# Six chunk lengths between 500 and 512 in place of five of 512 and one of 480, in a column attention followed by a two-layer block on one TensorE-bound core

## The chip, the cores and the metric

The kernel runs on one core of one Trainium2 chip. The metric is the device time of one execution in microseconds (us), from the start to the end of the program on that core; the time before is the median of three runs. A profiled execution gives, beside that, the time of each instruction on each engine: TensorE (PE, whose weight loads are listed apart as PEld), VectorE (DVE), ScalarE (ACT), GpSimd (POOL) and SyncE (SP), which issues the DMAs.

## The reference

```python
def _attn_ref(q, k, v, tau):                      # each (4, 6080, 256)
    qn = q / (np.linalg.norm(q, axis=1, keepdims=True) + 1e-06)
    kn = k / (np.linalg.norm(k, axis=1, keepdims=True) + 1e-06)
    s = kn.transpose(0, 2, 1) @ qn / tau          # (4, 256, 256)
    s = s - s.max(-1, keepdims=True)
    a = np.exp(s)
    a /= a.sum(-1, keepdims=True) + 1e-09
    return (v @ a).astype(np.float32)             # (4, 6080, 256)

def _moe_ref(x, w_in, w_out):                     # (24320, 256), (256, 2048), (2048, 256)
    h = x @ w_in
    g = h - np.tanh(h)
    return (g @ w_out).astype(np.float32)
```

The attention's result, reshaped to 24,320 tokens, is the second function's input. There are four batches of 6,080 tokens.

## The kernel before

**The algebra.** For each batch the 256 by 256 scores are made first. The softmax matrix is then multiplied into `w_in` (`fold`, tile `ps_w`), eight pieces of 256 hidden columns, so that `v` times the folded weight gives the hidden layer at once. That product is done by a seven-product scheme for two by two blocks (Winograd's form of Strassen's): the two columns of blocks on the moving side are two *chunks* of tokens, x and y, and the two rows are the two halves of the 256 channels. A *pair* of chunks of equal length `n` is therefore the unit of the work on tokens. All operands of these products are split into a high and a low part of a four-byte format with reduced precision, and each product takes three matmuls (high by low, high by high, low by high).

**Loops.** A batch is `NP = 6` pairs (list `pairs`, of start and length `n`), and a pair goes through `NS2 = 8` *slots*, one for each piece of the hidden layer. `gs` numbers the slots through all batches (192 in all). In a slot class `Quad` issues the seven products of the first layer (`products`, L288, tiles `x`, `y`, `z`; 21 matmuls of `n` columns), ACT and DVE add them up and apply h - tanh(h) (L805 to L845, tiles `u`, `p`, `c`, `t`, `gh`, `gl`), and `second` (L905, tiles `ps_o`) issues 24 matmuls of `n` columns into four accumulators that live through the eight slots. So a slot has 45 matmuls of `n` columns each, whatever `n` is. At the end of a pair the four accumulators are copied (L929) and written to `outT` (L940).

**Beside the slots.** Class `Moving` loads a pair's four blocks of `v` (`vraw`, L674), makes the sums (`vt`, L681 and L684) and splits all seven moving operands (L693 on ACT, L696 on DVE) some five slots before the pair begins. The next batch's scores (L288, tile `ps_s`, matmuls of 256 columns) and folds (`ps_w`, 256 columns) are strewn between the slots.

**Buffers.** Tiles for chunks are allocated for `NMAX = 512` columns whatever `n` is, and a shorter chunk uses the first `n` columns of each; a PSUM bank holds 512 columns of four bytes.

**What sets the order.** Class `Plan` records every operation with an estimated cost (`pe_cost`, `act_cost`, `dve_cost`, `pool_cost`, all linear in the number of columns), simulates the engines greedily with these costs, and issues the operations in the order of their simulated starts. The PE's own operations stay in the order in which they were recorded, but for the fills (parts of batch 1's scores), which may move among them. On the host, `kernel` lays out `v` so that a pair's four blocks lie side by side in a row of `v4`.

```python
s0 = 0
while s0 < N:
    n = min(NMAX, (N - s0) // 2)
    pairs.append((s0, n))
    s0 += 2 * n
```

With N = 6,080 this gives five pairs of 512 and one of 480.

Of the kernel before, what the change touches and what calls it, by code (L numbers as in the profile page):

```python
# [18 lines left out]
P = 128  # L19
GJ = 2  # L20
NMAX = 512
NSQ = 760
F64_LEAST = float(np.int32(0x38100000).view(np.float32))

# [204 lines left out]
def attn_moe(ctx: ExitStack, tc: tile.TileContext, qk, v4, qkT, tau, w_in, w_out, outT):  # L229
# [7 lines left out]
    B, N, _, C = qk.shape  # L237
# [3 lines left out]
    FB = 2 * P  # L241
    NJ = N // P
    TAIL = N - NJ * P
    pairs = []
    s0 = 0
    while s0 < N:
        n = min(NMAX, (N - s0) // 2)
        pairs.append((s0, n))
        s0 += 2 * n
    NP = len(pairs)  # L250
    SLOTS = NP * NS2
    TOTAL = B * SLOTS
# [17 lines left out]
    def sb(pool, tag, shape, dtype, name):  # L270
        return pool.tile(list(shape), dtype, tag=tag, name=name, bufs=ring[tag].bufs)

    def bank(i, name, shape=(P, 512)):

        return ps_p.tile(list(shape), F32, tag=f"bank{i}", name=name)
# [38 lines left out]
    class Convert:  # L314
# [10 lines left out]
        def magnitude(self):  # L325
            words = self.raw.rearrange("p a (n w) -> p (a n) w", w=2)
            self.low, self.high = words[:, :, 0], words[:, :, 1]
            self.a = sb(nt_p, "nt", [P, NSQ], I32, f"a_{self.name}")[:, 0:WN]
            self.af = self.a.bitcast(F32)
# [60 lines left out]
    while j < NJ:  # L390
        n = min(GJ, NJ - j) if j else NJ % GJ or GJ
# [7 lines left out]
    class Attn:  # L399
# [25 lines left out]
        def square_plain(self, g):  # L425
            j0, n, rows = groups[g]
            raw = self.parts[g]
            if g == 0:

                self.acc = [bank(i, f"acc{i}_{self.b}", (P, 2, C)) for i in (4, 3)]  # L430
                self.acc.append(sb(g_p, "t", [P, NMAX], F32, "acc").rearrange("p (x c) -> p x c", x=2))
                for a in self.acc[n:]:
# [14 lines left out]
        def take_squares(self, j):  # L447
            sq = sb(g_p, "u", [P, NMAX], F32, f"sq{j}").rearrange("p (x c) -> p x c", x=2)
            nc.scalar.copy(sq, self.acc[j])
            self.acc[j] = sq  # L450
# [25 lines left out]
        def split_hi(self, g):  # L476
            j0, n, rows = groups[g]
            raw = self.parts[g][0]
            hi = sb(qk_p, "qh", [P, GJ, 2, C], F32R, f"qh_{self.b}_{g}")
            nc.scalar.copy(hi[:rows, 0:n], raw[:rows, 0:n])  # L480
            self.parts[g] = [hi, raw]
# [26 lines left out]
        def load_channels(self, i):  # L508

            row, part = divmod(i, N // NSQ)  # L510
            self.channels[i] = sb(nt_p, "nt", [P, NSQ], F32, f"nt_{self.b}_{i}")
            nc.sync.dma_start(
                self.channels[i],
                qkT[row // KC, self.b, row % KC * P:(row % KC + 1) * P, part * NSQ:(part + 1) * NSQ],
            )

        def square(self, i):
            if i == 0:
                self.squares = sm_p.tile([P, 2 * KC, N // NSQ], F32, name="squares")
            x = self.channels.pop(i)  # L520
            row, part = divmod(i, N // NSQ)
            nc.scalar.activation(x, x, AF.Square, accum_out=self.squares[:, row, part:part + 1])
# [138 lines left out]
    class Moving:  # L661
# [9 lines left out]
        def load(self):  # L671
            n, s0 = self.n, self.s0
            self.raw = sb(v_p, "vraw", [P, 4, NMAX], F32, f"vraw_{self.b}_{self.p}")
            nc.sync.dma_start(self.raw[:, :, 0:n], v4[self.b, :, 2 * s0:2 * s0 + 4 * n].rearrange("p (a n) -> p a n", a=4))  # L674

        def sums(self, i):
            n = self.n
            r = self.raw[:, :, 0:n]
            if i == 0:
                self.t = sb(v_p, "vt", [P, 4, NMAX], F32, f"vt_{self.b}_{self.p}")  # L680
                nc.vector.tensor_sub(self.t[:, 0:2, 0:n], r[:, 1:3, :], r[:, 0:2, :])  # L681
# [8 lines left out]
        def split_hi(self, i):  # L690
            x = sb(v_p, "vhl", [P, 2, NMAX], F32R, f"v{i}_{self.b}_{self.p}")
            self.hi[i], self.lo[i] = (x[:, j, 0:self.n] for j in range(2))
# [466 lines left out]
    for gs in range(TOTAL):  # L1159
# [3 lines left out]
        for name, then in ORDER:  # L1163
# [6 lines left out]
            for x in then:  # L1170
                if isinstance(x, int):
                    lag, x = max(0, lag - x), max(0, x - lag)
# [48 lines left out]
```

## Time and profile before

| what | value |
|---|---|
| median of three runs | 2171.79 us (2171.21 to 2172.72) |
| profiled execution, first to last instruction | 2170.3 us |
| around that span (median less span) | 1.5 us |
| PE busy | 2160.4 us, 10,042 matmul records |
| DVE busy | 1750.3 us |
| ACT busy | 1529.9 us |
| mean granted TensorE clock | 0.998 |

The page gives no whole time of the profiled execution apart from its span, so sums made on the trace are set against 2170.3 us, and the difference is carried over to the median. Matmuls overlap, and the duration listed for one is longer than its share of the engine: what a matmul costs in a stream is read from the distance between starts in the timeline, and is called its *pitch* here.

### The profile page before, as it was taken

How to read it: one execution, taken by the hardware profiler on the slowest of the kernel's cores; microseconds unless marked ns; L12 is line 12 of the kernel's file. 1: busy time of each engine (PE TensorE's matmuls, PEld its weight loads, DVE VectorE, ACT ScalarE, POOL GpSimd, SP SyncE). 2: the span in 40 equal slices, each digit the busy share in tenths (PEclk: the TensorE clock that was granted, in tenths of full speed). 3: DMA queues.
4: the chain of work that ended last, by engine and by line, in shares of the span. 5: the costliest groups of instructions: out<-in, count | busy, mean ns of one | idle time of the engine just before them, and what ended most of it. 6: DMA issues, size and time to landing. Idle time of an engine off the chain costs nothing.

```text
span 2170.3 us, 28452 instructions
## 1 busy us (share of the span) xinstructions
PE 2160.4 (100%) x10042; PEld 1818.0 (84%) x10042; DVE 1750.3 (81%) x2844; ACT 1529.9 (70%) x2755; POOL 33.0 (2%) x31
## 2 busy tenths in 40 slices
PE   8999999999999999999999999999999999999999
PEld 7888888888888888888888888888888888888887
DVE  8888877888888777778788877877878878778776
ACT  6566778776777777776677767777667766666665
POOL 5100000000000000000000000000000000000000
PEclk9999999999999999999999999999999999999999
DMA  9844444443454444543345445454333342332331
GB/s 389 330 166 154 164 168 148 162 154 105 151 209 151 172 164 168 182 160 140 126 145 187 170 162 189 143 189 167 128 134 128 122 148 88 129 129 93 125 120 53
DMA packets 82783, 342.23 MB, mean 158 GB/s; under 512 B 9042, under 2 KB 13138, under 8 KB 80082
## 3 DMA queue, kind: packets, MB, share of 16 engines
q1 hardware_dynamic: 82642, 340.43, 43.3%
q8 instruction: 79, 1.29, 0.2%
q14 instruction: 62, 0.51, 0.1%
HBM read 281.94 MB, written 58.46 MB: 157 GB/s over the span
## 4 chain that ended last, share of the span: by engine, by line
PE 98%; DMA 1%; DVE 0%; SPq 0%; issue 0%; ACT 0%
PE ps_o L905 48%; PE x L288 24%; PE y L288 12%; PE ps_s L288 6%; PE z L288 6%; PE ps_w L288 2%; DMA qh<-qk_dram 0%; DMA vhl<-qk_dram 0%; PE ps_n L457 0%; DVE m_wi L346 0%; PE ps_b L564 0%; PE ps_t L599 0%; DVE acc L445 0%; DVE a_wi L339 0%; SPq L323 0%
## 5 line engine op out<-in xcount | busy, mean ns | idle before, releaser
L288 PE MATMUL x<-v,f 128*128 128x512 f32 (+1 forms) x2304 | 614.9, 388 | 0.0
L905 PE MATMUL ps_o<-gh,wo_h 128*128 128x512 f32 (+1 forms) x1536 | 596.8, 389 | 0.0
L905 PE MATMUL ps_o<-gh,wo_l 128*128 128x512 f32 (+1 forms) x1536 | 596.3, 388 | 0.0
L845 DVE TENSOR_TENSOR gl<-t,gh 128x512 fp32r<-128x512 f32 (+1 forms) x768 | 513.1, 681 | 57.3 <-ACT gh L841 55.3
L841 ACT CAST gh<-t 128x512 fp32r<-128x512 f32 (+1 forms) x768 | 463.7, 617 | 68.5 <-DVE t L837 61.2
L288 PEld LDWEIGHTS x<-v,f 128*128 128x128 f32 x2304 | 432.4, 188 | 87.4 <-issue 0.3
L905 PE MATMUL ps_o<-gl,wo_h 128*128 128x512 f32 (+1 forms) x1536 | 472.7, 389 | 0.0
L833 ACT ACTIVATE t<-c 128x512 f32<-128x512 f32 (+1 forms) x576 | 361.3, 628 | 134.0 <-DVE c L821 128.8
L837 DVE TENSOR_TENSOR t<-c,t 128x512 f32<-128x512 f32 (+1 forms) x576 | 392.5, 683 | 76.6 <-ACT t L833 69.0
L805 ACT COPY u<-x 128x512 f32<-128x512 f32 (+1 forms) x384 | 223.9, 583 | 236.7 <-PE x L288 235.7
L905 PEld LDWEIGHTS ps_o<-gh,wo_l 128*128 128x128 f32 x1536 | 288.5, 188 | 56.6 <-ACT gh L841 0.2
L905 PEld LDWEIGHTS ps_o<-gl,wo_h 128*128 128x128 f32 x1536 | 288.6, 188 | 55.3
L905 PEld LDWEIGHTS ps_o<-gh,wo_h 128*128 128x128 f32 x1536 | 288.7, 188 | 53.3
L821 DVE TENSOR_TENSOR c<-u,y 128x512 f32<-128x512 f32 (+1 forms) x384 | 261.0, 680 | 85.1 <-ACT u L805 51.4
L288 PE MATMUL y<-v,f 128*128 128x512 f32 (+1 forms) x1152 | 322.1, 388 | 0.0
L288 PEld LDWEIGHTS y<-v,f 128*128 128x128 f32 x1152 | 216.2, 188 | 43.1
L833 ACT ACTIVATE t<-x 128x512 f32<-128x512 f32 (+1 forms) x192 | 113.9, 593 | 114.7 <-PE x L288 113.5
L837 DVE TENSOR_TENSOR t<-x,t 128x512 f32<-128x512 f32 (+1 forms) x192 | 131.6, 685 | 72.9 <-ACT t L833 71.1
L821 DVE TENSOR_TENSOR c<-p,z 128x512 f32<-128x512 f32 (+1 forms) x192 | 130.9, 682 | 69.9 <-PE z L288 65.8
L288 PE MATMUL z<-v,f 128*128 128x512 f32 (+1 forms) x576 | 161.2, 388 | 0.0
L288 PEld LDWEIGHTS z<-v,f 128*128 128x128 f32 x576 | 108.1, 188 | 21.5
L805 ACT COPY p<-x 128x512 f32<-128x512 f32 (+1 forms) x192 | 112.0, 584 | 11.3 <-PE x L288 8.8
(122 smaller groups left out, 1490.4 us busy)
## 6 DMA issues: line engine op xcount, KB each, us to landing
f<-f_d SPq DMA_DIRECT2D x160, 896.0 KB, 4.6
nt<-qkT_dram SPq DMA_DIRECT2D x96, 380.0 KB, 5.7
f_d<-f SPq DMA_DIRECT2D x32, 896.0 KB, 3.8
raw<-qk_dram SPq DMA_DIRECT2D x46, 512.0 KB, 5.5
vraw<-v_dram SPq DMA_DIRECT2D x20, 1024.0 KB, 7.8
outT_dram<-ob SPq DMA_DIRECT2D x80, 256.0 KB, 3.1
wi<-wi_d SPq DMA_DIRECT2D x28, 512.0 KB, 5.4
vhl<-qk_dram SPq DMA_DIRECT2D x14, 512.0 KB, 8.9
```

Of the source, the lines that this page charges most:

```text
L288: ins = nc.tensor.matmul(out, w, x, start=first and i == 0, stop=last and i == len(seq) - 1, skip_group_check=True,)
L805: nc.scalar.copy(self.tiles[to], self.tiles["X"][:, 0:self.n])
L821: nc.vector.tensor_add(self.tiles[i], self.tiles[u], self.tiles[ps][:, 0:self.n])
L833: nc.scalar.activation(self.tiles["t", i], self.tiles[c][:, 0:n], AF.Tanh)
L837: nc.vector.tensor_sub(x, self.tiles[c][:, 0:n], x)
L841: nc.scalar.copy(self.g[i][0], self.tiles["t", i])
L845: nc.vector.tensor_sub(self.g[i][1], self.tiles["t", i], self.g[i][0].bitcast(F32))
L905: nc.tensor.matmul(outs[key + (m,)][:, 0:n], (wo_l if part else wo_h)[:, f, m * P:(m + 1) * P], quad.g[i][x], start=first and j == 0, stop ...
```

## The change

The lengths of the six pairs are written out. The sum stays at 3,040 columns for each side of a batch, and the number of pairs at six.

```diff
 NMAX = 512
+LENGTHS = 512, 510, 508, 506, 504, 500
...
-    pairs = []
-    s0 = 0
-    while s0 < N:
-        n = min(NMAX, (N - s0) // 2)
-        pairs.append((s0, n))
-        s0 += 2 * n
+    pairs = [(2 * sum(LENGTHS[:i]), n) for i, n in enumerate(LENGTHS)]
+    assert 2 * sum(LENGTHS) == N
...
-    for s0 in range(0, N, 2 * NMAX):
-        x, y = np.split(vT[:, :, s0:s0 + 2 * NMAX], 2, axis=2)
+    for i, n in enumerate(LENGTHS):
+        s0 = 2 * sum(LENGTHS[:i])
+        x, y = np.split(vT[:, :, s0:s0 + 2 * n], 2, axis=2)
```

The numbers of lines after `NMAX` are lower by three in the changed kernel (L902 is L905 of before, L285 is L288). On PE the order is the same through the whole program but for one place, at the passage from batch 0's first pair to its second. There stood before (`ps_o` are the second layer's accumulators, `ps_s` the next batch's scores, `x` a first product of the new pair; the shape is partitions by columns):

```order
L905 MATMUL ps_o_0_0_1_850<-gh_0_0_6_1567,wo_h 128x512
L905 MATMUL ps_o_0_0_1_850<-gl_0_0_6_1656,wo_h 128x512
L905 MATMUL ps_o_0_0_0_841<-gl_0_0_6_1656,wo_h 128x512
L288 MATMUL ps_s_455<-ql_21_1472 128x256 x2
L288 MATMUL ps_s_455<-qh_22_1499 128x256 x2
L288 MATMUL x_1_0_1638<-v_0_1_1659,f_1436 128x512 x3
```

and there stands now:

```order
L902 MATMUL ps_o_0_0_1_850<-gh_0_0_6_1567,wo_h 128x512
L285 MATMUL ps_s_455<-ql_21_1472 128x256 x2
L902 MATMUL ps_o_0_0_1_850<-gl_0_0_6_1673,wo_h 128x512
L902 MATMUL ps_o_0_0_0_841<-gl_0_0_6_1673,wo_h 128x512
L285 MATMUL ps_s_455<-qh_22_1499 128x256 x2
L285 MATMUL x_1_0_1638<-v_0_1_1660,f_1436 128x510 x3
```

Two score matmuls moved ahead of two matmuls of the second layer, and the new pair's products have 510 columns in place of 512.

DVE, whose results those matmuls read, has its operations in a slightly other order around each passage. In the same place it had before (`vt` and `v` are the next pair's sums and split operands, `c` the sum of two products, `gl` the low half that the second layer reads):

```order
L681 TENSOR_TENSOR vt_1_1618<-vraw_1_1057 128x1024
L696 TENSOR_TENSOR v_0_1_1115<-vraw_1_1057,v_0_1_1115 128x512
L821 TENSOR_TENSOR c_0_0_7_1630<-p_0_0_7_1536,z_0_7_1569 128x512
L821 TENSOR_TENSOR c_0_0_7_1636<-u_0_0_7_1609,y_0_7_1588 128x512
L684 TENSOR_TENSOR vt_1_1618<-vraw_1_1057,vt_1_1618 128x512
L845 TENSOR_TENSOR gl_0_0_6_1651<-t_0_0_6_1546,gh_0_0_6_1614 128x512
```

and has now:

```order
L678 TENSOR_TENSOR vt_1_1618<-vraw_1_1057 128x2x510
L818 TENSOR_TENSOR c_0_0_7_1626<-p_0_0_7_1536,z_0_7_1569 128x512
L693 TENSOR_TENSOR v_0_1_1115<-vraw_1_1057,v_0_1_1115 128x510
L818 TENSOR_TENSOR c_0_0_7_1636<-u_0_0_7_1609,y_0_7_1588 128x512
L681 TENSOR_TENSOR vt_1_1618<-vraw_1_1057,vt_1_1618 128x510
L842 TENSOR_TENSOR gl_0_0_6_1651<-t_0_0_6_1546,gh_0_0_6_1614 128x512
```

One addition of the running slot moved ahead of one split of the next pair's operands, and the two blocks in the first row are no longer one run of 1,024 columns.

## The prediction, made before the changed kernel ran

> **What bounds the kernel now.** I read the page's busy times and its chain of work first, then the groups by line and shape, the timeline of PE in three places, a table by stages, and last the waits, the DMAs and the tail. From the page:
>
> ```profile
> span 2170.3 us, 28452 instructions
> PE 2160.4 (100%) x10042; PEld 1818.0 (84%) x10042; DVE 1750.3 (81%) x2844; ACT 1529.9 (70%) x2755; POOL 33.0 (2%) x31
> PE 98%; DMA 1%; DVE 0%; SPq 0%; issue 0%; ACT 0%
> ```
>
> PE is busy in 2160.4 of 2170.3 us, and the chain that ended last is PE for 98% of the span (its third row here). So the time is the sum of the pitches of PE's matmuls, and any other engine counts only if it makes PE wait. How many matmuls the change touches follows from the code: 45 to a slot, 8 slots to a pair, 4 batches, so 1,440 for each of the six pairs. The groups by shape agree; the first product's tile has, for the two lengths,
>
> ```profile
> L288 PE MATMUL x<-v,f 128*128 128x512 f32 x1920 | 516.6, 390 | 0.0
> L288 PE MATMUL x<-v,f 128*128 128x480 f32 x384 | 99.4, 378 | 0.0
> ```
>
> that is five to one. All in all 7,200 matmuls have 512 columns and 1,440 have 480. The 390 and 378 ns are durations of overlapping matmuls and say little of the pitch. That comes from starts in the timeline of PE (columns: start, length, what). In a stretch of batch 0 in which nothing but slots runs, the `z` product, once in every slot, begins at
>
> ```profile
> 433.07 0.84 PE L288 MATMUL z<-v,f 128*128 128x512 f32 x3
> ...
> 443.27 0.84 PE L288 MATMUL z<-v,f 128*128 128x512 f32 x3
> ```
>
> and 45 matmuls lie between: 10.20 us / 45 = 226.67 ns for 512 columns. In the last pair of the last batch:
>
> ```profile
> 2122.12 0.81 PE L288 MATMUL z<-v,f 128*128 128x480 f32 x3
> ...
> 2131.87 0.81 PE L288 MATMUL z<-v,f 128*128 128x480 f32 x3
> ```
>
> 9.75 us / 45 = 216.67 ns for 480 columns. A fold gives a third length, 12 matmuls of 256 columns of the same four-byte format, from its first to the second layer's matmul that follows it:
>
> ```profile
> 96.15 0.40 PE L288 MATMUL ps_w<-wi,eh 128*128 128x256 f32 x2
> ...
> 97.23 0.40 PE L288 MATMUL ps_w<-wi,eh 128*128 128x256 f32 x2
> 97.47 0.28 PE L288 MATMUL ps_w<-wi,el 128*128 128x256 f32 x1
> 97.59 0.40 PE L905 MATMUL ps_o<-gh,wo_h 128*128 128x512 f32 x1
> ```
>
> 1.44 us / 12 = 120 ns. From 256 to 512 columns the pitch grows by 106.67 ns, 0.4167 ns a column. On that line 480 columns would cost 226.67 - 32 x 0.4167 = 213.33 ns. The trace has 216.67: **the short pair pays 3.33 ns a matmul more than the line.** The clock is no reason, as the table by stages (PE, PEld, DVE, ACT and POOL busy, then PEclk, DMA share and GB/s) shows for a stretch of 512 and the one of 480:
>
> ```profile
> 90.00:480.00 390.00, 390.00 (x1749) 323.82 (x1749) 322.39 (x533) 285.28 (x526) 0.00 (x0) 1.00 0.47 168
> 2080.00:2165.00 85.00, 85.00 (x391) 73.20 (x390) 60.48 (x99) 51.76 (x94) 0.00 (x0) 1.00 0.22 78
> ```
>
> Both have a granted clock of 1.00 and PE without a gap. What the 3.33 ns are decides this change, since five of the six pairs get lengths that the trace doesn't show.
>
> **The slots' matmuls, part by part.** The change adds no matmul and takes none away, and the columns are the same: 5 x 512 + 480 = 3,040 = 512 + 510 + 508 + 506 + 504 + 500. The slots now cost 7,200 x 226.67 + 1,440 x 216.67 = 1,944.0 us. The six pitches of before sum to 1,350 ns, and 1,440 matmuls of each make the same 1,944.0.
>
> By the line alone, the new lengths cost 226.67, 225.83, 225.00, 224.17, 223.33 and 221.67 ns: 1,346.67 ns, 1,939.2 us, so 4.8 us less than now. This is the lower bound of the slots' term: no row lies under the line.
>
> By a straight interpolation between the two neighbouring rows, 512 and 480 (0.3125 ns a column), the six cost 6 x 226.67 - 0.3125 x 32 = 1,350 ns, the same as now: 0.0 us.
>
> By a fixed price of 3.33 ns for every length that isn't whole in some unit of which 512 and 256 are multiples and 480 isn't (64, 128 or 256 columns), five of the six are dearer: 1,346.67 + 5 x 3.33 = 1,363.33 ns, 1,963.2 us, +19.2 us. This price would make 510, 508, 506 columns dearer than 512 (229.17 ns against 226.67 for 510). If 512 columns are the most that a matmul can cost, it is cut off there: 510, 508, 506 and 504 cost 226.67 (the line and 3.33 ns give at least that), 500 costs 225.00, and the sum is 5 x 226.67 + 225.00 = 1,358.33 ns, 1,956.0 us, **+12.0 us**.
>
> I take the last value. A price that came off a whole piece at once fits the three rows with one constant, while the interpolation needs the excess to shrink smoothly towards 512 and yet to be nothing at 256; and the new lengths lie 0 to 12 columns from the 512 row and 20 to 30 from the 480 row, so the 512 row's pitch is the nearer one. Both ends, -4.8 and +19.2, go into the range.
>
> The Trainium skill ("TensorE: Matmul & The Clock Gate", section "Back-to-back issue gap") gives a gap of N / 2.4 + 2.5 ns for matmuls in a row. Its slope is the one between the 256 and 512 rows here, but it puts 480 at 202.5 and 512 at 215.8, 13.3 ns apart, where the trace has 10.0; with its slope for every length the slots would lose 4.8 us, which is the rival on the line, below.
>
> **The order.** In PE's order two score matmuls change places with two of the second layer: the same work, 0 us. DVE and ACT get their work in a slightly different order at the passages. What hides this is their slack: in the 512 stretch above DVE is busy 322.39 of 390 us, 83%, and the widths shrink on all engines together. The costs by shape are
>
> ```profile
> L845 DVE TENSOR_TENSOR gl<-t,gh 128x512 fp32r<-128x512 f32 x640 | 431.0, 687 | 45.9 <-ACT gh L841 43.8
> L845 DVE TENSOR_TENSOR gl<-t,gh 128x480 fp32r<-128x480 f32 x128 | 82.1, 653 | 11.5 <-ACT gh L841 11.5
> L841 ACT CAST gh<-t 128x512 fp32r<-128x512 f32 x640 | 388.8, 622 | 55.3 <-DVE t L837 48.5 <-PE ps_o L905 6.1
> L841 ACT CAST gh<-t 128x480 fp32r<-128x480 f32 x128 | 75.0, 595 | 13.2 <-DVE t L837 12.7
> ```
>
> 1.06 ns a column on DVE and 0.84 on ACT, so a chunk of 500 columns costs some 20 ns more than one of 480 there, and one of 504 to 510 some 2 to 8 less than one of 512. A slot has 11 such DVE operations: at 500 in place of 480 that is 0.23 us of a 10 us slot. Cost 0; if the cover were gone at a passage, a late `gl` would hold PE for about one DVE operation, 0.7 us, at 24 passages at the worst 17 us. Little suggests it: of all the waits of PE's in slots for DVE or ACT, the longest row (total, times, longest) is
>
> ```profile
> PEld ps_o L905 <- ACT gh L841: 0.2, 1, 0.2
> ```
>
> and the planner's costs are linear in the columns.
>
> **The loads and stores.** SP issues as many DMAs as before. The load of a pair's `v` loses its single run of 8 KB a partition in four of the six pairs and becomes four runs of 2,000 to 2,040 bytes, and the rows written to `outT` begin at odd places. The trace has the four-run form already, in the 960 KB row:
>
> ```profile
> vraw<-v_dram SPq DMA_DIRECT2D x20, 1024.0 KB, 7.8
> outT_dram<-ob SPq DMA_DIRECT2D x80, 256.0 KB, 3.1
> vraw<-v_dram SPq DMA_DIRECT2D x4, 960.0 KB, 7.7
> outT_dram<-ob SPq DMA_DIRECT2D x16, 240.0 KB, 2.0
> ACT v L693 <- DMA vraw<-v_dram: 1.7, 1, 1.7
> ```
>
> The last number of a DMA row is us to landing: 7.7 for four runs, 7.8 for one. The last row, from the waits, is the only wait for `vraw` in the program (1.7 us, once, by ACT, off PE). The load is issued five slots, some 50 us, before its pair, so a second 8 us in landing would still lie beside slots: 0 us, from both sides.
>
> **The tail.** After the last matmul come a copy split between two engines and the last write:
>
> ```profile
> 2166.53 0.36 ACT L929 COPY ob<-ps_o 128x240 f32<-128x240 f32 x1 [0.74 <-PE ps_o L905]
> 2166.92 0.41 DVE L929 COPY ob<-ps_o 128x240 f32<-128x240 f32 x1 [0.39 <-ACT ob L929]
> ```
>
> With 250 columns in each half both grow by 10 columns, about 0.01 us each, and the write from 240 to 250 KB lands after 2.0 us (the row above) or at most the 3.1 of 256 KB: 0 to 1.1 us, taken as 0.1, nearest to the 240 KB row.
>
> **Sum.** +12.0 + 0 + 0 + 0.1 = +12.1 us on the profiled 2170.3 us: 2182.4. The median stands 1.5 us over that span, so 2171.8 + 12.1 = **2183.9 us**. About 0.2%, 4.3 us, is what a measurement can tell from no change.
>
> **Rivals.**
> - *On the line.* The 3.33 ns belong to 480 alone, by something in that length which none of the new ones has. For it: two rows of three, 256 and 512, fix a line. Against it: it leaves the third without a reason. -4.8 us, 2167.0: faster, and just over what can be told. This side decides if the mean pitch of the six is under 224.5 ns (225.0 less 4.3 us / 8,640).
> - *Interpolation.* The excess falls evenly from 480 to 512: 2171.8, no change. For it: nothing but the two nearest rows. The change then does nothing.
> - *Uncut price.* Lengths between pieces cost the line and 3.33 ns even over 512: 2191.0. It is the upper half of my own case.
> - *A growing price.* What is paid grows with the columns beyond the last whole 64 (32 of them cost 3.33 ns at 480, 0.104 each; 62, 60, 58, 56 and 52 would cost 6.5 to 5.4): 30 ns more over the six lengths, 43.2 - 4.8 = +38.4, 2210. It rests on one row and gives 510 a pitch of 232 ns.
> - *A wait at the passages*, as costed above: up to +17 us.
>
> **How the numbers follow.** My case with its two ends (+5 to +19.2) gets 0.40, the line 0.27, the interpolation 0.22, the growing price 0.06, the wait 0.03, other 0.02. Slower: 0.40 + 0.06 + 0.03 = 0.49. The line ends faster but for 0.02 that falls within 4.3 us: faster 0.25, and same 0.22 + 0.02 + 0.02 = 0.26. The range runs from the line's 2167.0 less 0.5 to the uncut 2191.0 plus 0.5, and leaves out the growing price and some of the waits; my own case alone has 2177 to 2191.
>
> **What would show it.** In the timeline of PE the distance between `z` products gives each length's pitch: my case wants 10.20 us a slot at 510 to 504 and 10.13 at 500; the line wants 10.16, 10.13, 10.09, 10.05 and 9.98; the uncut price 10.31, 10.28, 10.24, 10.20 and 10.13. The row for 512 must stay at 10.20. If slots are longer than their 45 pitches, with gaps before single matmuls, it is a wait. I am wrong if 510 costs clearly under 226 ns.

## The result, and the profile after

The changed kernel takes 2184.97 us (median of six runs), the kernel before 2172.2 in the same series: a ratio of 1.0056, 95% interval 1.0045 to 1.0067. It is slower by 12.8 us, where 12.1 were forecast. One of the six runs took 9125.32 us at a granted clock of 1.0, for a reason that the record does not show, and the ratio and its interval go by the other five. The page of the profiled execution:

```profile
span 2183.1 us, 28415 instructions
PE 2173.6 (100%) x10042; PEld 1819.6 (83%) x10042; DVE 1748.6 (80%) x2844; ACT 1531.7 (70%) x2755; POOL 33.0 (2%) x31
PE 98%; DMA 1%; SPq 0%; issue 0%; DVE 0%; ACT 0%
```

The span grew by 2183.1 - 2170.3 = 12.8 us and PE's busy time by 13.2, with the same 10,042 records. DVE and ACT moved by 2 us. PE's idle time did not grow (9.9 us before, 9.5 now). Summed over the whole trace from each matmul's start to the next one's, the slots' 8,640 matmuls took 1958.0 us before and take 1970.5 now, and all others 208.7 and 209.2: the loss lies in the slots. The timeline of PE, at the same kind of places as before (starts of the `z` product in slots without other matmuls, 45 matmuls apart):

```profile
229.51 0.84 PE L285 MATMUL z<-v,f 128*128 128x510 f32 x3
239.71 0.84 PE L285 MATMUL z<-v,f 128*128 128x510 f32 x3
...
321.59 0.85 PE L285 MATMUL z<-v,f 128*128 128x508 f32 x3
331.83 0.84 PE L285 MATMUL z<-v,f 128*128 128x508 f32 x3
...
383.02 0.84 PE L285 MATMUL z<-v,f 128*128 128x506 f32 x3
393.22 0.84 PE L285 MATMUL z<-v,f 128*128 128x506 f32 x3
...
464.80 0.84 PE L285 MATMUL z<-v,f 128*128 128x504 f32 x3
475.00 0.84 PE L285 MATMUL z<-v,f 128*128 128x504 f32 x3
...
546.59 0.84 PE L285 MATMUL z<-v,f 128*128 128x500 f32 x3
556.79 0.84 PE L285 MATMUL z<-v,f 128*128 128x500 f32 x3
...
2113.46 0.83 PE L285 MATMUL z<-v,f 128*128 128x500 f32 x3
2123.51 0.83 PE L285 MATMUL z<-v,f 128*128 128x500 f32 x3
```

A slot of 510, 506 and 504 columns takes 10.20 us, to the last digit what 512 columns take; 508 take 10.24, and 500 take 10.20 in some stretches and 10.05 in others. From one matmul to the next, the distances in the slots of 504 and 506 are 226 or 227 ns throughout, as they are in slots of 512: no single matmul is held up. With eight slots in four batches the six lengths cost 32 x (4 x 10.20 + 10.24 + 10.05 to 10.20) = 1954.9 to 1959.7 us, against 32 x (5 x 10.20 + 9.75) = 1944.0 before: +10.9 to +15.7, and the span's 12.8 lies between. The loads and the tail did what was expected of them (issue, count, KB, us to landing; then the waits; then the last two copies):

```profile
vraw<-v_dram SPq DMA_DIRECT2D x4, 1020.0 KB, 7.4
vraw<-v_dram SPq DMA_DIRECT2D x4, 1012.0 KB, 8.2
vraw<-v_dram SPq DMA_DIRECT2D x4, 1000.0 KB, 8.1
outT_dram<-ob SPq DMA_DIRECT2D x16, 255.0 KB, 3.5
outT_dram<-ob SPq DMA_DIRECT2D x16, 250.0 KB, 2.1
...
ACT v L690 <- DMA vraw<-v_dram: 2.4, 1, 2.4
DVE vt L678 <- DMA vraw<-v_dram: 0.2, 1, 0.2
...
2179.32 0.37 ACT L926 COPY ob<-ps_o 128x250 f32<-128x250 f32 x1 [0.77 <-PE ps_o L902]
2179.72 0.42 DVE L926 COPY ob<-ps_o 128x250 f32<-128x250 f32 x1 [0.40 <-ACT ob L926]
```

The four-run loads land in 7.4 to 8.2 us where one run took 7.8 before, and the only waits for one are 2.4 us of ACT's and 0.2 of DVE's, each once.

### The profile page after: what moved, and what is told of

Same layout as the page of the kernel before. It is cut to its first block, busy times and chain, and to the rows that moved or that the text cites. A ratio compares the mean times of both kernels' runs of the same rounds, so it can differ in the third digit from the quotient of the medians.

```text
span 2183.1 us, 28415 instructions
## 1 busy us (share of the span) xinstructions
PE 2173.6 (100%) x10042; PEld 1819.6 (83%) x10042; DVE 1748.6 (80%) x2844; ACT 1531.7 (70%) x2755; POOL 33.0 (2%) x31
## 4 chain that ended last, share of the span: by engine, by line
PE 98%; DMA 1%; SPq 0%; issue 0%; DVE 0%; ACT 0%
PE ps_o L902 48%; PE x L285 24%; PE y L285 12%; PE ps_s L285 6%; PE z L285 6%; PE ps_w L285 2%; DMA vhl<-qk_dram 1%; DMA ql<-qk_dram 0%; PE ps_n L454 0%; PE ps_b L561 0%; PE ps_t L596 0%; SPq L462 0%; SPq L320 0%; DVE ob L926 0%; ACT ob L926 0%
## 5 line engine op out<-in xcount | busy, mean ns | idle before, releaser
L285 PE MATMUL x<-v,f 128*128 128x512 f32 (+5 forms) x2304 | 618.7, 390 | 0.0
L902 PE MATMUL ps_o<-gh,wo_l 128*128 128x510 f32 (+5 forms) x1536 | 598.1, 389 | 0.0
L902 PE MATMUL ps_o<-gh,wo_h 128*128 128x510 f32 (+5 forms) x1536 | 598.0, 389 | 0.0
L842 DVE TENSOR_TENSOR gl<-t,gh 128x512 fp32r<-128x512 f32 (+5 forms) x768 | 512.1, 680 | 57.2 <-ACT gh L838 55.2
L838 ACT CAST gh<-t 128x512 fp32r<-128x512 f32 (+5 forms) x768 | 464.1, 618 | 67.1 <-DVE t L834 64.7
L285 PEld LDWEIGHTS x<-v,f 128*128 128x128 f32 x2304 | 432.6, 188 | 90.2 <-issue 0.3
L902 PE MATMUL ps_o<-gl,wo_h 128*128 128x510 f32 (+5 forms) x1536 | 474.5, 390 | 0.0
L830 ACT ACTIVATE t<-c 128x512 f32<-128x512 f32 (+5 forms) x576 | 361.5, 628 | 132.7 <-DVE c L818 126.6
L834 DVE TENSOR_TENSOR t<-c,t 128x512 f32<-128x512 f32 (+5 forms) x576 | 391.5, 682 | 77.1 <-ACT t L830 69.4
L902 PEld LDWEIGHTS ps_o<-gh,wo_l 128*128 128x128 f32 x1536 | 288.7, 188 | 58.6 <-ACT gh L838 0.2
L902 PEld LDWEIGHTS ps_o<-gl,wo_h 128*128 128x128 f32 x1536 | 288.6, 188 | 56.9
L902 PEld LDWEIGHTS ps_o<-gh,wo_h 128*128 128x128 f32 x1536 | 288.8, 188 | 55.3
L285 PE MATMUL y<-v,f 128*128 128x510 f32 (+5 forms) x1152 | 323.8, 389 | 0.0
L818 DVE TENSOR_TENSOR c<-u,y 128x506 f32<-128x506 f32 (+5 forms) x384 | 260.7, 679 | 77.1 <-ACT u L802 47.7
L285 PEld LDWEIGHTS y<-v,f 128*128 128x128 f32 x1152 | 216.3, 188 | 44.9
L285 PE MATMUL z<-v,f 128*128 128x512 f32 (+5 forms) x576 | 161.9, 389 | 0.0
L285 PEld LDWEIGHTS z<-v,f 128*128 128x128 f32 x576 | 108.2, 188 | 22.5
```

What stands on the lines that cost most here:

```text
L285: ins = nc.tensor.matmul(out, w, x, start=first and i == 0, stop=last and i == len(seq) - 1, skip_group_check=True,)
L818: nc.vector.tensor_add(self.tiles[i], self.tiles[u], self.tiles[ps][:, 0:self.n])
L830: nc.scalar.activation(self.tiles["t", i], self.tiles[c][:, 0:n], AF.Tanh)
L834: nc.vector.tensor_sub(x, self.tiles[c][:, 0:n], x)
L838: nc.scalar.copy(self.g[i][0], self.tiles["t", i])
L842: nc.vector.tensor_sub(self.g[i][1], self.tiles["t", i], self.g[i][0].bitcast(F32))
```

## The experiments

Two theories stood after the timeline. *Fixed price*, the forecast's: the pitch is the line through 256 and 512 columns plus 3.33 ns for any length that is no multiple of 64, cut off at the pitch of 512. *Steps*: the pitch is that of the number of columns rounded up to a multiple of 16, on the same line, that is 13.33 ns + 0.4167 ns a rounded column; what 480 pays beyond its step (216.67 against 213.33 ns) is then a thing of its own. Beside them: the order, and the loads.

**The order undone.** The changed lengths, with the planner's costs reckoned for the old ones, so that every engine has the old order:

```diff
+PLANNED = 512, 512, 512, 512, 512, 480
...
-            plan.add("ACT", act_cost(n), tanh, reads=[self.bufs[c]], writes=[t])
+            plan.add("ACT", act_cost(self.m), tanh, reads=[self.bufs[c]], writes=[t])
...
```

(`self.m` is the pair's entry of `PLANNED`, and it stands in every cost that took a chunk's length.)

> The changed lengths, but the planner's costs are reckoned with 512 five times and 480, so that every engine has the order of the kernel before. If the 12.8 us lie in the matmuls' pitch, this takes the changed kernel's 2185 within 2 us. If the changed order makes waits, it comes out below that by what the order cost, down to 2172.

Measured: 2184.62 us, ratio to the kernel before 1.006 (1.0047 to 1.0072). In its trace PE, DVE and ACT run their operations in the order of the kernel before, from the first to the last. The order costs nothing that can be told.

**The load undone.** The changed kernel, with the four blocks of `v` side by side in the buffer, so that a load is one run again:

```diff
-            self.raw = sb(v_p, "vraw", [P, 4, NMAX], F32, f"vraw_{self.b}_{self.p}")
+            raw = sb(v_p, "vraw", [P, 4, NMAX], F32, f"vraw_{self.b}_{self.p}")
+            self.raw = raw.rearrange("p a n -> p (a n)")[:, 0:4 * n].rearrange("p (a n) -> p a n", a=4)
```

> The changed kernel with a pair's four blocks of v side by side in the buffer, so that each load is one run a partition again, as before the change; no other buffer moves. If the form of the load costs nothing, the changed kernel's 2185 within 2 us. If the 34 us that the kernel with rows 520 columns apart lost came from its loads, part of the 12.8 us goes away here, down to 2172.

Measured: 2184.69 us, ratio 1.0057 (1.0043 to 1.0071). The form of the load costs nothing either. (The 34 us in the expectation are told below, under the place of the operands.) What is left is the length.

**Multiples of 16.**

```diff
-LENGTHS = 512, 510, 508, 506, 504, 500
+LENGTHS = 512, 512, 512, 512, 496, 496
```

> Lengths 512, 512, 512, 512, 496, 496. Fixed price (the line through 256 and 512, plus 3.33 ns for any length that is no multiple of 64, at most the pitch of 512): 496 columns take 220.00 + 3.33 = 223.33 ns, six pitches 1353.33 ns, +4.8 us on the kernel before: about 2177. Rounding up to whole 16 columns: 496 is whole and takes 220.00 ns, -4.8 us: about 2167. Interpolation between 480 and 512: 221.67 ns, no change, 2172.

Measured: 2171.27 us, ratio 0.9997 (0.9988 to 1.0006): the same as before, which is near neither sum and is the number that interpolation gave. But interpolation wanted one pitch, 221.67 ns or 9.98 us a slot, and no slot has it: the timeline shows two. Most slots of 496 columns without other matmuls take 9.90 us, 220.00 ns a matmul, as steps want it (fixed price: 10.05); but six of 27 take 10.05, and those with six score matmuls of 256 columns, 0.72 us, among them take 10.76 in place of 10.62:

```profile
451.55 0.82 PE L285 MATMUL z<-v,f 128*128 128x496 f32 x3
461.45 0.82 PE L285 MATMUL z<-v,f 128*128 128x496 f32 x3
...
541.19 0.83 PE L285 MATMUL z<-v,f 128*128 128x496 f32 x3
551.24 0.83 PE L285 MATMUL z<-v,f 128*128 128x496 f32 x3
...
978.68 0.83 PE L285 MATMUL z<-v,f 128*128 128x496 f32 x3
989.44 0.83 PE L285 MATMUL z<-v,f 128*128 128x496 f32 x3
```

So an exact multiple of 16 can pay half a step (3.33 ns) more, as 480 does, and here that took back most of the 4.8 us.

**A ladder of lengths.** Three kernels with seven pairs each, read for the pitch and not for the time. They stand for the edits of one line: `LENGTHS = 448, 464, 472, 496, 488, 384, 288`, then `498, 494, 490, 486, 482, 320, 270`, then `478, 476, 474, 470, 466, 340, 336`.

> Seven pairs of 448, 464, 472, 496, 488, 384 and 288 columns, read for the pitch of each length. Fixed price: 200.00, 210.00, 213.33, 223.33, 220.00, 173.33 and 136.67 ns. Rounding up to whole 16 columns: 200.00, 206.67, 213.33, 220.00, 220.00, 173.33 and 133.33 ns. A price that needs a whole multiple of 128 puts 448 at 203.33. The time as a whole, 1440 matmuls more of each kind, is about 2211 by the fixed price, more if ACT or DVE hold PE at the short lengths.

> Seven pairs of 498, 494, 490, 486, 482, 320 and 270 columns, read for the pitch of each. Fixed price: 224.17, 222.50, 220.83, 219.17, 217.50, 146.67 and 129.17 ns. Rounding up to whole 16 columns: 226.67, 220.00, 220.00, 220.00, 220.00, 146.67 and 126.67 ns. The line alone: 220.83, 219.17, 217.50, 215.83, 214.17, 146.67 and 125.83 ns.

> Seven pairs of 478, 476, 474, 470, 466, 340 and 336 columns, read for the pitch of each. Steps of 16: 213.33 ns for the first five alike (216.67 if what 480 pays beyond its step is paid on the whole step), 160.00 for 340, 153.33 for 336. Fixed price: 215.83, 215.00, 214.17, 212.50, 210.83, 158.33 and 156.67 ns.

They took 2207.38, 2216.46 and 2205.46 us, one run each. From the timelines of the second and third:

```profile
286.65 0.82 PE L285 MATMUL z<-v,f 128*128 128x490 f32 x3
296.55 0.82 PE L285 MATMUL z<-v,f 128*128 128x490 f32 x3
```

```profile
201.89 0.80 PE L285 MATMUL z<-v,f 128*128 128x476 f32 x3
211.49 0.80 PE L285 MATMUL z<-v,f 128*128 128x476 f32 x3
...
1757.08 0.80 PE L285 MATMUL z<-v,f 128*128 128x478 f32 x3
1766.68 0.80 PE L285 MATMUL z<-v,f 128*128 128x478 f32 x3
```

490 columns cost what 496 do, and 476 and 478 cost 9.60 us a slot, 213.33 ns, *less* than a slot of 480 costs in the kernel before (9.75). All lengths, by distances between `z` products without other matmuls between:

| columns | pitch by steps, ns | measured, ns |
|---|---|---|
| 512, 510, 506, 504, 498 | 226.67 | 226.67 |
| 508 | 226.67 | 227.6 |
| 500 | 226.67 | 223.33 or 226.67 |
| 496 | 220.00 | 220.00, at times 223.33 |
| 494 | 220.00 | 223.3 |
| 488 | 220.00 | 225.7 |
| 490, 486, 482 | 220.00 | 220.00 |
| 480 | 213.33 | 216.67 |
| 478, 476, 474, 472, 470, 466 | 213.33 | 213.33 |
| 464 | 206.67 | 208.9 |
| 448 (one stretch) | 200.00 | 206.67 |
| 384, 336, 320, 270 | 173.33, 153.33, 146.67, 126.67 | the same |
| 340, 288 | 160.00, 133.33 | 155.0, 131.7 |

Steps give most rows exactly; fixed price, which wanted 217.50 for 482 and 210.83 for 466 (both a whole step's price instead), falls. The rest lie within half a step, on either side, but for 488 and 448 above and 340 below.

The traces show one thing more about the rows that are off, in the single distances between starts. At 494 columns they are 218 and 228 ns by turns, at 500 in the slots of 10.05 us 221 and 226. At 464 they repeat after three matmuls, at 340 and 288 after four, at 508 and 488 after seven. Each time the repeated run adds up to a whole number of steps of 6.67 ns: 67 for two matmuls of 494 or of 500, 65 for two of 480, 94 for three of 464, 93 and 79 for four of 340 and of 288, 239 and 237 for seven of 508 and of 488 (one slot of 340, with a gap before a matmul, left out). So the pitches in the table are means over a slot, a half step is an odd step shared by two matmuls, and no row is off the grid of 6.67 ns once its run is taken whole. Why a run takes that number of steps and not the one of the rounded length (31 for one matmul of 448, where rounding gives 30) stays open. Each matmul here has a weight load before it (PEld, 83% busy); whether these take part was not tried.

**Two columns moved.**

```diff
-LENGTHS = 512, 510, 508, 506, 504, 500
+LENGTHS = 512, 512, 512, 512, 510, 482
```

> Lengths 512, 512, 512, 512, 510, 482: the kernel before with two columns moved from one pair of 512 to that of 480. Steps of 16: 510 stays at 226.67 and 482 takes 220.00 in place of 216.67 ns, +4.8 us, about 2177. Fixed price: 217.50 ns for 482, +1.2 us, 2173. Smooth: no change, 2172.

Measured: 2176.28 us against 2172.58, ratio 1.0018 (1.0009 to 1.0027), +3.7 us. The sign and most of the size are the steps'; the interval, +2.0 to +5.9 us, leaves out the 1.2 of the fixed price and no change. Its slots of 482 columns are at 9.90 us, where the fixed price wanted 9.79:

```profile
2105.79 0.82 PE L285 MATMUL z<-v,f 128*128 128x482 f32 x3
2115.69 0.82 PE L285 MATMUL z<-v,f 128*128 128x482 f32 x3
```

**Padding.** The changed pairs, every chunk filled up with zeros to 512 columns:

```diff
-            self.s0, self.n = pairs[p]
+            self.s0, self.n = NMAX * 2 * p, NMAX
...
-            self.n = pairs[self.p][1]
+            self.n = NMAX
...
+        x, y = (np.pad(a, ((0, 0), (0, 0), (0, NMAX - n))) for a in (x, y))
```

> The changed pairs, each chunk padded with zeros to 512 columns: every engine works on 512 columns in all six pairs (3,072 a side and batch in place of 3,040), and only the true columns are stored. If a matmul is paid in whole steps of 16 columns, the padding of 510 to 504 is free and the whole takes what the changed kernel takes, 2185 to 2187 (500 columns go from 223.33 or 226.67 to 226.67 ns). If the pitch followed the columns in any smooth way, 32 x 0.4167 x 1440 ns = 19 us more than the changed kernel, about 2204.

Measured: 2186.14 us, ratio 1.0064 (1.0051 to 1.0077), 1.2 us over the changed kernel (0.8 by the differences to the kernel before, each in its own series) where a smooth pitch would have been 19 over it. The changed kernel had paid for nearly all of these 32 columns a batch and side already.

**Where the operands lie.** A control for the loads came out far from both expectations. The kernel before, with the rows of `v`'s buffer 520 columns apart, so that its loads are four runs:

```diff
-            self.raw = sb(v_p, "vraw", [P, 4, NMAX], F32, f"vraw_{self.b}_{self.p}")
+            self.raw = sb(v_p, "vraw", [P, 4, NMAX + 8], F32, f"vraw_{self.b}_{self.p}")
```

> The kernel before, with rows of the buffer for v 520 columns apart, so that each load of v lands in four runs of 2,048 bytes a partition in place of one, as in the changed kernel. If the loads are hidden, no change, 2172 within 2 us. If they took part in the 12.8 us, slower by their part.

Measured: 2206.96 us, ratio 1.0158 (1.0143 to 1.0174). The edit had also pushed the buffers that are allocated behind this one 128 bytes on. So the push was tried alone, with the loads as before:

```diff
     const.tile([P, PAD], F32, name="pad")
+    g_p.tile([P, 32], F32, name="shift", bufs=1)
```

> The kernel before with an unused 128 bytes a partition ahead of the second layer's buffers: gh, gl, the folded weights f and all behind them lie 128 bytes later, v and the loads are as before. If the place of the operands sets the pitch, about 2206, as with the rows 520 columns apart, and 10.43 us a slot at 512 columns. If that loss came from the loads, 2172.

Measured: 2207.07 us, ratio 1.0159 (1.0146 to 1.0173). It is the place: PE, DVE and ACT run in the same order as before, `gl` on DVE still takes 687 ns and `gh` on ACT 622, and PE's longest wait in a slot for either is 0.2 us as before. The timeline of PE of this last kernel:

```profile
428.73 0.88 PE L288 MATMUL z<-v,f 128*128 128x512 f32 x3
439.16 0.88 PE L288 MATMUL z<-v,f 128*128 128x512 f32 x3
```

10.43 us a slot for the same 512 columns; the distances from start to start run from 224 to 241 ns, where they were 226 or 227. With a push of 512 bytes (128 elements in place of 32):

> The kernel before, with gh, gl, f and all behind them 512 bytes later in place of 128. If any place off a multiple of 2048 bytes costs what 128 did, about 2207 and 10.43 us a slot of 512 columns. If multiples of 512 bytes are as good, 2172 and 10.20 us.

Measured: 2172.31 us, ratio 1.000 (0.999 to 1.001), and 10.20 us a slot:

```profile
431.98 0.84 PE L288 MATMUL z<-v,f 128*128 128x512 f32 x3
442.18 0.84 PE L288 MATMUL z<-v,f 128*128 128x512 f32 x3
```

Last, whether the steps count columns or the aligned pieces that they touch: lengths 512 four times and 496 twice, as above, with the 496 columns put 8 columns into each buffer that TensorE streams:

```diff
+            o = 8 if self.n == 496 else 0
-            self.hi[i], self.lo[i] = (x[:, j, 0:self.n] for j in range(2))
+            self.hi[i], self.lo[i] = (x[:, j, o:o + self.n] for j in range(2))
...
```

(and the same for `gh` and `gl`.)

> Lengths 512 four times and 496 twice, with the 496 columns of each moving operand (v, gh, gl) put 8 columns into their buffers. If a matmul is paid by the number of its columns rounded up to 16, no change against the same lengths without the offset, 2171. If it is paid by the aligned pieces of 16 columns that it touches, 496 columns touch 32 pieces and cost 226.67 in place of 220.00 ns, up to +19 us: 2190.

Measured: 2175.57 us against 2171.27 without the offset (ratios to the kernel before 1.0014, 1.0005 to 1.0023, and 0.9997). The slots that took 9.90 us still do:

```profile
2105.13 0.82 PE L285 MATMUL z<-v,f 128*128 128x496 f32 x3
2115.03 0.82 PE L285 MATMUL z<-v,f 128*128 128x496 f32 x3
```

and those at 10.05 are at 10.10. So in the slots of 9.90 us the steps go by the number of columns; the place adds something of its own in some stretches.

## Why the prediction was right

**What bounds the kernel**: right. PE's busy time took all of the loss, and order and loads, costed at nothing, cost nothing when each was undone alone.

**The cut at 512's pitch**: right, and it carried the result. 510, 506 and 504 cost 226.67 ns as the sum had them; 508 cost 0.9 ns more, 500 lay on both sides of the 225.00.

**The reason under it**: wrong. The step that failed is "a fixed price of 3.33 ns for every length that isn't whole". It gave 10.20 us for 506 to 510 only through the cut (504 came to 226.67 ns by the price itself), and further down it fails: 482 and 490 columns both cost 220.00 ns, where it wanted 217.50 and 220.83; 478 to 466 all cost 213.33, where it wanted 215.83 down to 210.83. What the runs showed in its place are steps: most lengths cost what the next multiple of 16 costs on the line. The 3.33 ns at 480, from which the price was made, are not the price of being no multiple of 64: 496 is none either, and 21 of its 27 slots without other matmuls don't pay them.

That 12.1 came within 0.7 us of the 12.8 is therefore in part luck. Six lengths at whole steps would have cost 32 x 6 x 10.20 - 1944.0 = +14.4 us; the forecast stood lower through a price for 500 columns (225.00 ns) that none of their slots has, and the measured loss through slots of 500 at 10.05 us and, it seems, score matmuls that cost a little less beside the shorter chunks (six of them 0.72 us at 510, 0.74 at 512).

**The line** (the rival that ended faster) fails by the slots of 504 to 510: 10.20 us where it wanted 10.05 to 10.16. With it falls, for these matmuls, the linear gap of N / 2.4 + 2.5 ns in the Trainium skill ("TensorE: Matmul & The Clock Gate", "Back-to-back issue gap"), which that section calls the isolated gap, without the weight loads that stand here (10,042 of them, one to a matmul). Its slope joins the tops of the steps, and within a step most lengths cost the same: 226.67 ns at 510 and at 498 columns, 220.00 at 490 and at 482. *Interpolation*, *uncut price* and *growing price* fail by the same rows; a *wait at the passages* would have gone with the old order.

**The tail**: right within 0.1 us; the two halves of the last copy grew by 0.01 us each.

## What to carry to other kernels

On a TensorE-bound kernel count a split by the steps that its matmuls pay, not by its columns: here most lengths in a stream of these four-byte matmuls are paid in sixteens, so evening out 512 and 480 to 510 ... 500 came to nearly the price of 32 columns of padding, 12.8 us. Read a matmul's price from the distance between starts in the timeline, at several lengths, before shifting columns about; two lengths always look like a line. And when an edit changes a buffer's size, look at what lies behind it before blaming the edit.

No version here beat the kernel before beyond what can be told; 512 four times and 496 twice came out the same.

## What was unexpected of the hardware

The place of operands in on-chip memory can change TensorE's pitch: 128 bytes of shift under `gh`, `gl`, `f` and all that lies behind them made a slot of 512 columns take 10.43 in place of 10.20 us and the kernel 34.5 us slower (2207.07 against 2172.55), while 512 bytes cost nothing. Which of the shifted operands does it wasn't tried. And the same length can run at two pitches half a step apart in one execution, 500 columns at 10.05 and 10.20 us a slot, the first with two matmuls sharing an odd step; what chooses between them stays open.
